# Truer durations in a build-time planner: layer norm, transposes, mixer output, normalisation products and TensorE's change of mode

## The chip, the core and the metric

The kernel runs on one core of one Trainium2 chip. The metric is the device time of one execution in microseconds. A timed comparison runs the two kernels in turn on the same chip.

## The reference, cut to what matters

Two layers, each an attention block followed by a token-mixing MLP, with S = 2048 tokens, D = 640 channels, 32 heads of 20 channels, F = 1536.

```python
x = x + A(layernorm(x), wqkv, wo)         # softmax(q k^T / sqrt(20)) v, then wo
x = x + B(layernorm(x), w1, b1, w2, b2)   # gelu over mixed tokens, residual
x = x + A(layernorm(x), wqkv, wo)         # the same weights again
x = x + B(layernorm(x), w1, b1, w2, b2)
```

## The kernel before

The instructions of each engine are not written down in an order. They are emitted by a greedy planner that runs while the program is built. It keeps a clock for each engine, gives every job a duration, and at each step emits the job that can start first on its engine. On the chip nothing of these clocks is left. What is left is the order in which each engine's instructions stand in the program, and the semaphores that they wait on.

```python
PE_MM = 216.0      # planned ns of one matmul of 512 columns
SW = 100.0         # planned ns for a change of TensorE's tiling mode
LAT_V = 120.0      # planned ns from VectorE's end to the reader
HAM_MIN = 10.0     # below this much recent matmul work, a hole gets a filler
...
def run_until(done):
    while not done():
        best = None
        for ch in (act_choose, dve_choose, pe_choose, pool_choose, sp_choose):
            c = ch()
            if c is not None and (best is None or c[0] < best[0]):
                best = c
        best[1](best[0])          # emits the instructions, advances that clock
```

The exponentials of the softmax are the largest work. They are cut in *units* of 128 keys x 512 queries x 4 heads, that is four *chunks* of 512 columns. ScalarE takes two or three chunks in one activation. The planner gives whole units to VectorE instead when it expects VectorE to finish them in time. VectorE then makes four *conversions* of scores and five *term passes*, whose results TensorE adds up.

```python
# ScalarE: n = 2 or 3 chunks
nc.scalar.activation(out=P[:, 0:n, :]..., in_=St[:, 0:n, :]..., func=ACT.Exp, scale=SCALE)
end = start + 67 + 426.7 * n
...
# VectorE: a conversion, and a term pass
nc.vector.tensor_scalar(out=c["jt"][:, j*512:(j+1)*512], in0=Dt[:], scalar1=..., scalar2=..., op0=ALU.mult, op1=ALU.add)
end = start + 600
...
nc.vector.tensor_scalar(out=tt_[:], in0=c["jt"][:], scalar1=0.5, scalar2=TERM_C[i], op0=ALU.mult, op1=ALU.add)
end = start + 605
...
# is one more unit worth giving to VectorE?
eta = (max(clk["DVE"], clk["PE"]) + (4 * 600.0 + NTERM * 610.0) * (d["open"] + 1) + len(t_jobs) * 610.0
       + sum(e[3] for e in jobs["DVE"]) + D_SLACK)
if eta <= act_end(si): ...
```

Where the planner sees a hole of over 250 ns on TensorE and little matmul work in the last 3.4 us, it emits a *filler*: a matmul with a zero weight, which adds nothing to an open accumulator. There are 362 fillers, 10 of them at the start.

TensorE works in three tiling modes: scores in four row groups, products with V and most others in four column groups, some at full size.

The softmax here doesn't subtract the row's maximum and nothing guards it: scores larger than these inputs give would overflow.

## Time and profile before

| | before |
|---|---|
| median of 4 runs | 1739.62 us (1738.45 to 1740.51) |
| span of the profiled execution | 1738.1 us |
| exponentials of layer 0, first start to last end | 782.3 us |
| change-over (mixer, next layer's start) | 50.2 us |
| exponentials of layer 1, first start to last end | 810.2 us |
| after the last exponential | 75.4 us |

From the profile's page: the span, the engines' busy time with its share of the span, and the chain of waits by engine.

```profile
span 1738.1 us, 50479 instructions
...
PE 1660.4 (96%) x21922; PEld 640.6 (37%) x21923; DVE 1463.7 (84%) x2613; ACT 1590.3 (91%) x1436; POOL 183.2 (11%) x297
...
PE 48%; ACT 21%; DVE 19%; issue 9%; DMA 2%; POOL 1%; DVEq 0%; POOLq 0%; SPq 0%; ACTq 0%
```

No engine stands out, so the averages must be split by stage. The next view is busy time in windows. The columns are: window and its width; busy us (and instructions) of PE, PEld, DVE, ACT, POOL; granted clock; DMA share; GB/s. The windows are layer 0's exponentials, the change-over, layer 1's first part (to the 37th accumulator transpose), layer 1's rest, and the tail.

```profile
20.00:802.30 782.30, 751.09 (x10025) 266.26 (x10018) 700.51 (x1227) 763.35 (x677) 84.07 (x117) 1.00 0.15 43
802.30:852.50 50.20, 47.07 (x475) 30.38 (x475) 28.08 (x66) 23.40 (x36) 6.70 (x20) 0.97 0.33 101
852.50:999.50 147.00, 142.16 (x2511) 69.53 (x2510) 73.67 (x146) 127.97 (x124) 12.05 (x27) 1.00 0.22 68
999.50:1662.70 663.20, 636.83 (x8317) 219.96 (x8314) 614.61 (x1064) 650.44 (x571) 68.63 (x96) 0.99 0.18 56
1662.70:1738.10 75.40, 69.04 (x517) 48.30 (x516) 33.35 (x70) 12.83 (x16) 3.66 (x12) 0.97 0.34 101
```

Read the width against ScalarE's busy time. Layer 0 leaves ScalarE idle for 782.30 - 763.35 = 18.95 us, layer 1's rest for 12.8 us. There ScalarE binds, and an idle microsecond of it is a microsecond of the kernel. In the change-over and layer 1's first part TensorE binds.

The durations that the change corrects stand in the groups by shape (mean ns of one after the comma):

```profile
L976 DVE STREAM_TRANSPOSE T_85<-pst 128x512 f32<-128x512 f32 x54 | 38.1, 705 | 2.6 <-PE pst L927 2.6
L1011 DVE STREAM_TRANSPOSE attnT<-T_86 128x256 f32<-128x256 f32 x62 | 26.6, 431 | 3.6 <-POOL T_86 L1001 3.5
L343 DVE BATCH_NORM_STATS2 bnst<-xs 128x6 f32<-128x320 f32 x40 | 19.1, 478 | 0.0
L1392 DVE SCALAR_TENSOR_TENSOR xs<-pst,b_t,xs 128x320 f32<-128x320 f32 x24 | 13.1, 550 | 34.0 <-PE pst L456 29.3 <-PE pst L453 3.3 <-DMA x2d<-xs 1.0
L530 DVE TENSOR_SCALAR attnT<-xs,mv,rt 128x640 bf16<-128x640 f32 x16 | 9.8, 612 | 7.9 <-POOL rt L356 7.8
L1001 POOL TENSOR_TENSOR T_86<-T_85,rden 128x512 bf16<-128x512 f32 x62 | 65.9, 1063 | 1132.7 <-DVE rden L988 1090.5 <-DVE attnT L1011 42.2
```

The cost of a change of mode shows in TensorE's timeline (start, duration of a run of matmuls, what ran):

```profile
1634.09 0.39 PE L700 MATMUL pst<-QT,KT 32*128 32x512 bf16 x2
1634.40 0.39 PE L927 MATMUL pst<-P,Vaug 128*32 128x512 bf16 x2
1634.41 0.39 PE L927 MATMUL pst<-JT,Vaug 128*32 128x512 bf16 x2
1634.63 0.85 PE L1065 MATMUL pst<-wo,attnT 128*32 128x320 bf16 x20
```

From the products at 1634.40 to the next group in the same mode is 0.23 us. From the scores at 1634.09 to the products, a change of mode, is 0.31 us. The difference is 0.08 us here. Over the whole trace, outside its half-clock stretches, the medians of the same two intervals are 225 and 321 ns, so a change of mode costs some 0.1 us.

### The profile page before, as it was taken

The page shows a single profiled execution, that of the slowest core. Times are in us where ns is not written, and L with a number is a line of the kernel's source. Part 1 is how long each engine was busy: PE and PEld are TensorE (multiplying, and loading weights), DVE is VectorE, ACT ScalarE, POOL GpSimd, SP SyncE. Part 2 cuts the span into 40 slices and gives each one's busy share as a digit, 9 for nine tenths or more (in the row PEclk, how much of TensorE's full clock was granted, in tenths as well). Part 3 has the DMA queues.
Part 4 walks back from the last instruction along what each step waited for, and adds up shares of the span by engine and source line. Part 5 has one row for each costly group of instructions (what it writes and reads, how often), then busy time and mean ns, then how long its engine had stood idle before and what let it go on. Part 6 is the DMA issues. An engine that isn't in the chain of part 4 may idle for free.

```text
span 1738.1 us, 50479 instructions
## 1 busy us (share of the span) xinstructions
PE 1660.4 (96%) x21922; PEld 640.6 (37%) x21923; DVE 1463.7 (84%) x2613; ACT 1590.3 (91%) x1436; POOL 183.2 (11%) x297
## 2 busy tenths in 40 slices
PE   8999999999999999998999999999999999999989
PEld 3433333323333333335545423332233333333356
DVE  6588999999988889997444699999999888889963
ACT  7899999999999999997598799999999999999950
POOL 3100002000300021001101000210002000300010
PEclk9999999999999999999999999999999999999999
DMA  3200001000121105610522000100002120266133
GB/s 118 29 2 2 2 13 36 1 1 2 52 70 56 38 32 178 191 47 28 162 84 68 15 2 2 39 24 2 2 19 69 56 64 24 78 192 198 63 99 96
DMA packets 103295, 98.06 MB, mean 56 GB/s; under 512 B 45600, under 2 KB 79520, under 8 KB 103072
## 3 DMA queue, kind: packets, MB, share of 16 engines
q1 hardware_dynamic: 99456, 94.82, 17.7%
q8 instruction: 171, 2.80, 0.7%
q0 software_dynamic: 3616, 0.01, 0.3%
q14 instruction: 52, 0.43, 0.1%
HBM read 63.35 MB, written 31.46 MB: 55 GB/s over the span
## 4 chain that ended last, share of the span: by engine, by line
PE 48%; ACT 21%; DVE 19%; issue 9%; DMA 2%; POOL 1%; DVEq 0%; POOLq 0%; SPq 0%; ACTq 0%
ACT P L887 21%; PE pst L700 14%; PE pst L927 13%; PE pst L456 12%; DVE JT L860 7%; DVE JT L840 6%; PE pst L453 5%; PE pst L1065 3%; DVE T_85 L976 1%; PE pst L1483 1%; DMA W<-in_B_w_dram 1%; DVE attnT L1011 1%; DVE QT L463 0%; DMA uacc_74<-W 0%; DVE xs L1094 0%
## 5 line engine op out<-in xcount | busy, mean ns | idle before, releaser
L887 ACT ACTIVATE P<-pst 128x1536 bf16<-128x1536 f32 (+1 forms) x1336 | 1523.5, 1294 | 31.4 <-PE pst L700 15.3
L860 DVE TENSOR_SCALAR JT<-JT 128x2048 uint16<-128x2048 uint16 x945 | 636.0, 706 | 3.9 <-PE pst L927 0.2
L700 PE MATMUL pst<-QT,KT 32*128 32x512 bf16 (+1 forms) x4224 | 589.8, 376 | 36.3 <-ACT P L887 26.5
L840 DVE TENSOR_SCALAR JT<-pst 128x512 uint16<-128x512 f32 x756 | 504.0, 678 | 81.1 <-PE pst L700 78.2
L927 PE MATMUL pst<-P,Vaug 128*32 128x512 bf16 (+1 forms) x3444 | 503.9, 380 | 3.7 <-ACT P L887 1.9
L927 PE MATMUL pst<-JT,Vaug 128*32 128x512 bf16 (+1 forms) x3900 | 464.0, 379 | 4.9 <-DVE JT L860 2.4
L700 PEld LDWEIGHTS <-KT 32*128 32x128 bf16 x4224 | 165.5, 91 | 504.5 <-issue 492.8
L927 PEld LDWEIGHTS <-Vaug 128*32 128x32 bf16 x7344 | 170.9, 94 | 307.1 <-issue 275.6
L1001 POOL TENSOR_TENSOR T_86<-T_85,rden 128x512 bf16<-128x512 f32 x64 | 67.7, 1057 | 1157.1 <-DVE rden L988 1114.9
L1065 PE MATMUL pst<-wo,attnT 128*32 128x320 bf16 x2048 | 108.1, 304 | 7.1 <-DVE attnT L1011 3.9
L1483 PE MATMUL pst<-ident,zw 128*32 128x512 bf16 (+1 forms) x352 | 113.5, 374 | 0.0
L456 PEld LDWEIGHTS <-W 128*32 128x32 bf16 x3384 | 91.0, 96 | 59.8 <-issue 27.7
L456 PE MATMUL pst<-hh,wq 128*32 128x512 bf16 x1232 | 102.2, 381 | 2.2 <-DVE JT L840 1.7
L456 PE MATMUL pst<-hh,wk 128*32 128x512 bf16 x1240 | 95.2, 381 | 1.3 <-DVE JT L840 0.6
L456 PE MATMUL pst<-x1last,W 128*32 128x320 bf16 x1536 | 81.5, 301 | 0.8 <-DVE JT L840 0.4
L1065 PEld LDWEIGHTS <-attnT 128*32 128x32 bf16 x2048 | 51.7, 96 | 49.1 <-issue 26.8
L456 PE MATMUL pst<-attnT,hh 128*32 128x320 bf16 x1196 | 61.4, 300 | 2.5 <-DVE JT L840 0.8
L456 PE MATMUL pst<-JT,W 128*32 128x320 bf16 x1080 | 51.8, 300 | 0.0
L456 PE MATMUL pst<-hh,W 128*32 128x320 bf16 x768 | 43.2, 304 | 5.1 <-DMA W<-in_B_w_dram 3.7
L463 DVE CAST KT<-pst 128x512 bf16<-128x512 f32 x51 | 34.7, 679 | 15.9 <-PE pst L456 14.6
L976 DVE STREAM_TRANSPOSE T_85<-pst 128x512 f32<-128x512 f32 (+1 forms) x58 | 39.9, 688 | 7.0 <-PE pst L927 7.0
L354 POOL TENSOR_SCALAR rt<-mv 128x1 f32<-128x1 f32 x64 | 13.0, 203 | 310.9 <-DVE mv L346 309.9
(92 smaller groups left out, 878.3 us busy)
## 6 DMA issues: line engine op xcount, KB each, us to landing
W<-in_B_w_dram SPq DMA_DIRECT2D x10, 768.0 KB
W<-in_B_w_dram SPq DMA_DIRECT2D x24, 256.0 KB
xs<-in_A_x_dram SPq DMA_DIRECT2D x32, 160.0 KB
x2d<-xs SPq DMA_DIRECT2D x16, 320.0 KB
xs<-x2d SPq DMA_DIRECT2D x16, 320.0 KB
x1d_69<-xs SPq DMA_DIRECT2D x12, 320.0 KB
uacca_72<-W SPq DMA_DIRECT2D x12, 320.0 KB
W<-uacca_72 SPq DMA_DIRECT2D x12, 320.0 KB
```

Source lines behind the costliest of these rows:

```text
L453: nc.tensor.matmul(out_, lhsT=lhsT, rhs=rhs, start=start, stop=stop)
L456: nc.tensor.matmul(out_[32 * c:32 * c + 32], lhsT=lhsT[:, 32 * c:32 * c + 32], rhs=rhs, start=start, stop=stop, tile_position=(0, 32 * c))
L463: nc.vector.tensor_copy(out=out_, in_=in_)
L700: pe(nc.tensor.matmul(dst, lhsT=k_, rhs=q_, start=True, stop=True, tile_position=(32 * j, 0)))
L840: nc.vector.tensor_scalar(out=c["jt"][:, j * 512:(j + 1) * 512], in0=Dt[:], scalar1=SCALE * LOG2E * 256.0, scalar2=127.0 * 256.0, op0=ALU. ...
L860: nc.vector.tensor_scalar(out=tt_[:], in0=c["jt"][:], scalar1=0.5, scalar2=TERM_C[i], op0=ALU.mult, op1=ALU.add)
L887: nc.scalar.activation(out=P[:, 0:n, :].rearrange("p a b -> p (a b)"), in_=St[:, 0:n, :].rearrange("p a b -> p (a b)"), func=ACT.Exp, scal ...
L927: pe(nc.tensor.matmul(dst, lhsT=Vaug[:, n:n + 32], rhs=ap, start=acc["cnt"][j] == 1 and not part, stop=last[j] and (half is None or part = ...
L976: nc.vector.transpose(out=T1[:], in_=src[:, 0:w])
L1001: eng.tensor_tensor(out=o_, in0=a_, in1=b_, op=ALU.mult)
L1065: nc.tensor.matmul(t[32 * c:32 * c + 32, 0:w], lhsT=q_, rhs=wo_pad[:, gg, c0:c1], start=(gi == 0), stop=(gi == len(gs) - 1), tile_position ...
L1483: pe(nc.tensor.matmul(dst[0:32, 0:128 * n], lhsT=zw[:, 0:32], rhs=ident[:].unsqueeze(1).to_broadcast([128, n, 128]), start=not inside, sto ...
```

## The change

The intent is a plan that is nearer to the chip, so that the emitted order fits better. No instruction's work changes. The diff, cut to its core:

```diff
-SW = 100.0
+SW = 105.0
...                                        # layer norm: statistics of a token tile
-            then(mv, start + 950 + LAT_V)
-        push("DVE", prio, ready, 950, f)
+            then(mv, start + 1030 + LAT_V)
+        push("DVE", prio, ready, 1030, f)
...                                        # layer norm: scaling (450 in both places before)
+                cost = 530 if L.x_in_dt == F32 else 400
...                                        # transpose of the accumulator
-                    acc["ready"] = start + 720 + LAT_V
+                    acc["ready"] = start + 740 + LAT_V
...                                        # normalisation product on GpSimd
-                        end_ = start + (600 if final else 1450)
+                        end_ = start + (600 if final else 1200)
...
-                        push("POOL", 0, start + 150 + LAT_V, 1300, f_mul, ok=lambda: len(rT2) > 0)
+                        push("POOL", 0, start + 170 + LAT_V, 1050, f_mul, ok=lambda: len(rT2) > 0)
...                                        # second transpose
-                        push("DVE", 3, end_, 340, f_tr2, ...)
+                        push("DVE", 3, end_, 360, f_tr2, ...)
...                                        # mixer output
-                    add_fill(mms, 136.0, evac, 450.0, pr=...)
+                    add_fill(mms, 136.0, evac, 470.0, pr=...)
```

## The prediction

> **What bounds the kernel now.** The page of the profile: span 1738.1 us, TensorE busy 96%, ScalarE 91%, VectorE 84%, GpSimd 11%, clock near full. The chain of waits: 48% TensorE, 21% ScalarE exponentials, 19% VectorE. By stage (busy time in windows, timeline of ScalarE):
> - attention of layer 0, 20 to 802 us: exponentials bind, 98 to 99% busy from 200 us on, about 19 us idle in all; TensorE is 96 to 98% busy, VectorE 86 to 99%.
> - mixer and the next layer's start, 802 to 852 us: TensorE binds (46 of 50 us).
> - layer 1's first 150 us: TensorE binds (95.5% at 900 to 1000 us; ScalarE idles 19 us there).
> - then exponentials again to 1663 us; last, 75 us of mixer tail, TensorE alone.
>
> **What the change does.** No arithmetic changes. A clock that exists only while the program is built orders instructions; it gets durations nearer to the trace's. By groups: statistics of a token tile 1.12 us end to end (0.95 becomes 1.03); scaling 0.61 us from float32, 0.44 from bf16 (0.45 becomes 0.53 or 0.40); normalisation product on GpSimd 1.06 us (1.30 becomes 1.05); transposes 0.705 and 0.43; mixer output 0.55 (0.45 becomes 0.47). Neighbours overlap, so intervals are about 0.08 us under these. Before a change of TensorE's mode a 0.22 us matmul slot lasts 0.32 in the timeline, so 105 ns is as right as 100. The Trainium skill, "TensorEngine Tiling (Array Packing)", Key Properties, says that a change of mode drains TensorE; the trace agrees (about 0.1 us).
>
> The corrections sum to little: 64 x 0.08 + 62 x 0.02 + 66 x 0.02 + 64 x 0.02 + 0.5 = about 9 us of planned VectorE time, 2750 x 0.005 = 14 us of planned TensorE time. Real durations do not move; only the order can pay.
>
> **What moves.** Comparing the two orders: ScalarE, GpSimd and SyncE keep 97 to 99% of theirs; VectorE keeps half in place and TensorE a third, by local swaps. In layer 1 one more unit of exponentials goes to VectorE (945 to 950 term passes, 756 to 760 conversions): ScalarE saves 4 x 0.43 = 1.7 us; VectorE gets 9 x 0.6 = 5.4 us, and has room. One term pass now stands just before the last accumulator transpose. TensorE loses 34 filler matmuls (362 to 328), 23 of them short ones of the last group: fewer planned holes. It makes 14 fewer mode changes, 1.4 us. At equal numbers of score chunks, its other work differs by a few us at most. No large shift to gain from.
>
> **On the critical path.** Layer 0: same split, -1 +-3 us. Transition: 0 +-2. Layer 1: -2 +-3 (the unit, the mode changes). Tail: 0, same order. Sum: about -3 us.
>
> **Predicted: 1736.5 us, range 1730 to 1743.** Faster by over 2%: 1%; within 2%: 98%; slower by over 2%: 1%.
>
> **What would show it.** Layer 0's last exponential (802.3 us) moves by under 4 us; 802 to 852 us by under 2; layer 1's exponentials (811 us, first to last) shorten by 1 to 5; the tail stays at 75 us. Mean durations of all groups stay. GpSimd's change shows nowhere.
>
> **What would make it wrong.** The order is greedy and sensitive: a late VectorE pass at a group's end can stall TensorE and ScalarE, several times, for 5 to 10 us. Real exponentials run 2.286 us a pair against 2.268 planned, uncorrected here, so the plan still drifts, which may hide any gain. The extra unit can come late and add 1 to 2 us.

## The result, and the profile after

| | before | after |
|---|---|---|
| median, first comparison | 1739.62 us (4 runs) | 1738.05 us (4 runs, 1736.88 to 1743.37) |
| ratio after to before | | 0.9997, 95% interval 0.9975 to 1.0019 |
| median, repeated in a later batch (experiment 1) | 1737.33 us (9 runs) | 1735.94 us (5 runs) |
| ratio | | 0.9996, 95% interval 0.9982 to 1.0009 |

A ratio is the mean time of one kernel's runs over that of the other's of the same rounds, so it is not quite the ratio of the medians. The change leaves the time as it was: both intervals hold 1.

The profiled execution after, from its page:

```profile
span 1735.1 us, 50465 instructions
...
PE 1647.8 (95%) x21920; PEld 645.9 (37%) x21921; DVE 1461.4 (84%) x2624; ACT 1584.5 (91%) x1433; POOL 180.2 (10%) x297
...
PE 43%; ACT 25%; DVE 20%; issue 11%; DMA 2%; POOL 1%; SPq 0%; ACTq 0%; POOLq 0%; DVEq 0%
```

The same five windows after:

```profile
20.50:806.90 786.40, 750.31 (x10026) 268.89 (x10019) 697.70 (x1227) 762.40 (x676) 81.11 (x117) 0.99 0.15 43
806.90:857.80 50.90, 47.02 (x475) 30.46 (x475) 28.13 (x67) 22.95 (x33) 7.32 (x20) 0.97 0.32 100
857.80:1003.60 145.80, 141.59 (x2505) 70.62 (x2504) 73.46 (x146) 126.69 (x123) 12.08 (x27) 1.00 0.22 69
1003.60:1659.00 655.40, 626.58 (x8311) 221.66 (x8312) 614.20 (x1071) 647.44 (x571) 65.43 (x92) 0.99 0.18 55
1659.00:1735.10 76.10, 67.98 (x527) 47.94 (x522) 34.01 (x73) 12.83 (x16) 5.99 (x16) 1.00 0.38 111
```

A net of nothing hides two movements of opposite sign. Layer 0 became 4.1 us longer: ScalarE's idle time there rose from 18.95 to 24.0 us. Layer 1 became 9.0 us shorter (147.0 + 663.2 before, 145.8 + 655.4 after). In its rest ScalarE idles 8.0 us instead of 12.8 and works 647.4 us instead of 650.4. The tail became 0.7 us longer, at a higher granted clock.

This is one trace of each kernel. They differ by 3.0 us, the timed medians only by 1.6 and 1.4 us. TensorE's clock differs too: the traces' clock records list stretches of 3.41 us at half clock (called *half-clock windows* below), and layer 0 has none of them before and three after. What they are worth is taken up in experiment 7 and after experiment 12.

Of the groups shown above, those of VectorE keep their means within 3 ns; the product on GpSimd went from 1063 to 1094 ns:

```profile
L977 DVE STREAM_TRANSPOSE T_85<-pst 128x512 f32<-128x512 f32 x54 | 38.3, 708 | 1.3 <-PE pst L928 1.2
L1012 DVE STREAM_TRANSPOSE attnT<-T_86 128x256 f32<-128x256 f32 x62 | 26.7, 434 | 5.4 <-POOL T_86 L1002 4.9
L530 DVE TENSOR_SCALAR attnT<-xs,mv,rt 128x640 bf16<-128x640 f32 x16 | 9.8, 612 | 8.3 <-POOL rt L356 7.9
L1002 POOL TENSOR_TENSOR T_86<-T_85,rden 128x512 bf16<-128x512 f32 x62 | 67.9, 1094 | 1123.8 <-DVE rden L989 1081.7 <-DVE attnT L1012 42.1
```

Not every group kept its mean: the scaling from bf16 went from 444 to 484 ns, the exponentials from 1505 to 1529 and from 1084 to 1106 ns. The interval between two exponentials that run back to back stayed at 1331 and 904 ns.

How the tail begins shows in the timelines of ScalarE and VectorE. A row merges neighbours, names the first one's shape, and its duration runs to the end of the last. Before:

```profile
1659.36 3.32 ACT L887 ACTIVATE P<-pst 128x1024 bf16<-128x1024 f32 x3
...
1660.76 0.21 DVE L346 BATCH_NORM_AGGREGATE mv<-bnst 128x2 f32<-128x12 f32 x1
1663.17 0.45 DVE L976 STREAM_TRANSPOSE T_85<-pst 128x256 f32<-128x256 f32 x1 [2.20 <-PE pst L927]
```

After:

```profile
1656.06 2.89 ACT L888 ACTIVATE P<-pst 128x1536 bf16<-128x1536 f32 x3
...
1659.37 0.64 DVE L861 TENSOR_SCALAR JT<-JT 128x2048 uint16<-128x2048 uint16 x1
1660.51 0.45 DVE L977 STREAM_TRANSPOSE T_85<-pst 128x256 f32<-128x256 f32 x1 [0.50 <-PE pst L928]
```

Before, the last exponential ends at 1662.68 and the last accumulator is transposed 0.49 us later; VectorE had been waiting. After, the last exponential ends at 1658.95, but a term pass of the extra unit on VectorE runs to 1660.01, TensorE must still use it, and the transpose starts 1.56 us after the exponential.

### The profile page after: what moved, and what is told of

It reads as the page before. It is cut to its first block, busy times and chain, and to the rows that moved or that the text cites. A ratio compares the mean times of both kernels' runs of the same rounds, so it can differ in the third digit from the quotient of the medians.

```text
span 1735.1 us, 50465 instructions
## 1 busy us (share of the span) xinstructions
PE 1647.8 (95%) x21920; PEld 645.9 (37%) x21921; DVE 1461.4 (84%) x2624; ACT 1584.5 (91%) x1433; POOL 180.2 (10%) x297
## 4 chain that ended last, share of the span: by engine, by line
PE 43%; ACT 25%; DVE 20%; issue 11%; DMA 2%; POOL 1%; SPq 0%; ACTq 0%; POOLq 0%; DVEq 0%
ACT P L888 24%; PE pst L701 12%; PE pst L928 11%; PE pst L456 11%; DVE JT L861 8%; DVE JT L841 7%; PE pst L453 5%; PE pst L1066 2%; DMA W<-in_B_w_dram 1%; DVE T_85 L977 1%; PE pst L1484 1%; DMA x2d<-xs 0%; PE pst L542 0%; DVE QT L463 0%; DVE attnT L1012 0%
## 5 line engine op out<-in xcount | busy, mean ns | idle before, releaser
L701 PE MATMUL pst<-QT,KT 32*128 32x512 bf16 (+1 forms) x4224 | 577.9, 377 | 48.9 <-ACT P L888 37.2
L841 DVE TENSOR_SCALAR JT<-pst 128x512 uint16<-128x512 f32 x760 | 509.5, 681 | 86.3 <-PE pst L701 83.4
L701 PEld LDWEIGHTS <-KT 32*128 32x128 bf16 x4224 | 173.0, 91 | 522.1 <-issue 509.8
L1002 POOL TENSOR_TENSOR T_86<-T_85,rden 128x512 bf16<-128x512 f32 x64 | 69.4, 1084 | 1146.4 <-DVE rden L989 1104.2
L1484 PE MATMUL pst<-ident,zw 128*32 128x512 bf16 (+1 forms) x318 | 106.9, 381 | 0.0
L456 PEld LDWEIGHTS <-wk 128*32 128x32 bf16 x1240 | 33.0, 95 | 33.7 <-issue 18.0
```

The costliest lines, as they stand in the source:

```text
L456: nc.tensor.matmul(out_[32 * c:32 * c + 32], lhsT=lhsT[:, 32 * c:32 * c + 32], rhs=rhs, start=start, stop=stop, tile_position=(0, 32 * c))
L701: pe(nc.tensor.matmul(dst, lhsT=k_, rhs=q_, start=True, stop=True, tile_position=(32 * j, 0)))
L841: nc.vector.tensor_scalar(out=c["jt"][:, j * 512:(j + 1) * 512], in0=Dt[:], scalar1=SCALE * LOG2E * 256.0, scalar2=127.0 * 256.0, op0=ALU. ...
L1002: eng.tensor_tensor(out=o_, in0=a_, in1=b_, op=ALU.mult)
L1484: pe(nc.tensor.matmul(dst[0:32, 0:128 * n], lhsT=zw[:, 0:32], rhs=ident[:].unsqueeze(1).to_broadcast([128, n, 128]), start=not inside, sto ...
```

## The experiments

Four theories were set against each other.

- *Accuracy*: a plan nearer to the truth runs faster. Then the parts of the change gain too, and wrong constants lose.
- *Units*: the time follows how many units VectorE takes off ScalarE, at 4 x 0.43 = 1.7 us each.
- *The draw*: any nudge of the planner gives another order. Its quality has no fixed relation to the truth of the constants, but it belongs to the order, so it repeats from run to run and from program to program.
- *The clock*: the new order has fewer fillers, and TensorE's granted clock falls to half more often.

The stage figures below are read from one trace for each program, as in the windows above; "layer 1" is from its first exponential's start to its last one's end. Experiments 1 to 4, 5 to 8 and 9 to 12 are three batches on three chips, each timed against before on its own chip; stage figures are compared across them.

### 1. after_again: the changed kernel once more

No edit.

> The changed kernel unchanged, for its scatter and a second trace. If the first trace's stages are a property of the order, the second trace shows layer 0's exponentials (first to last) 786 us plus or minus 2, layer 1's 801 plus or minus 2, and the fast runs average 0.15% below before (about 1737). If the scatter of the first four runs (1736.9 to 1743.4) is a property of the clock, the slower runs show the lower granted clock, and the two traces differ where half-clock spells fall.

Measured: ratio 0.9996 (0.9982 to 1.0009). Layer 0 784.3 us, layer 1 801.2 us. Its five runs are 1734.19 and 1734.23 (clock 0.992), 1735.94 and 1736.62 (0.992) and 1740.08 (0.988). The stages repeat: layer 0 is again longer than before's (by 2.0 us) and layer 1 shorter (by 9.0 us). How much of the loss in layer 0 is the clock's is taken up after experiment 12. The expected 0.15% is not shown; the interval allows it. The slowest run is the one of the lowest clock.

### 2 and 3. sw_alone and costs_alone: the change in two parts

```diff
 # sw_alone: before, and only
-SW = 100.0
+SW = 105.0
 # costs_alone: after, and only
-SW = 105.0
+SW = 100.0
```

> Only the change of mode at 105 ns. In the built program this gives two more units to VectorE than before (955 term passes). Theory of accuracy (a plan nearer the truth runs faster): between before and after, ratio 0.998 to 1.000. Theory of units (time follows ScalarE's chunks): layer sums of exponentials 2 x 1.7 us shorter, ratio 0.998. Theory of the draw (any nudge gives another order, good or bad by luck): anywhere in 0.996 to 1.004, no relation to the sum of the parts.

> All of the change but the mode cost (100 ns). 955 term passes as well. Accuracy: ratio 0.998 to 1.000, and together with sw_alone the two parts sum to the whole (0.9985 or so). Units: 0.998. Draw: 0.996 to 1.004, parts do not sum.

Measured: sw_alone 1.0012 (0.9994 to 1.0030), costs_alone 0.9994 (0.9979 to 1.0009). Both give VectorE two more units than before. For the theory of units both should have come to 0.998; sw_alone's interval excludes it. Layer 0 took 784.5 and 780.7 us, change-over and layer 1 together 858.1 and 854.5 us (before 860.4, after 852.1). The parts do sum to the whole within the scatter, so this pair doesn't speak for the draw. It doesn't separate accuracy from the draw either.

### 4. mirror: every constant as far off the other way

```diff
-SW = 100.0                                   +SW = 95.0
-  950 (statistics)                           +  870
-  450 / 450 (scaling, float32 / bf16)        +  370 / 500
-  720, 340 (transposes)                      +  700, 320
-  1300, end 1450 (product on GpSimd)         +  1550, end 1700
-  450 (mixer output)                         +  430
```

(The diff is abridged: each line stands for the places of the change's own diff.)

> Every constant of the change moved as far from before's value, the wrong way (statistics 870, product 1550, transposes 700 and 320, mixer output 430, mode 95 ns). The built program gives four more units to VectorE (965 term passes). Accuracy: slower than before, ratio 1.001 to 1.005. Units: four units less on ScalarE, up to 4 x 1.7 = 7 us, ratio 0.996. Draw: 0.996 to 1.004 without a sign.

Measured: 1.0015 (1.0001 to 1.0028). As a whole this is what accuracy expected, and far from the 0.996 of units. By stage it isn't so simple. Layer 0 took 778.6 us, the shortest of any order here. Change-over and layer 1 took 859.5 us, the tail 78.7 us, at a mean granted clock of 0.9905 over the four runs. The wrong constants made the better layer 0: two of the four units are taken off ScalarE there (1652 chunks instead of 1660 in the trace). Its activations, each at its back-to-back interval, sum to 738.1 us in layer 0 against before's 742.0, which is the whole of the 3.7 us. With the other two, change-over and layer 1 took 859.5 us against 860.4.

### 5. after_shadow: more fillers, nothing else moved

```diff
+        if o[0] > now + 250 and now > 2000 and a.want:       # a planned hole before the chosen job
+            return (o[0], lambda s_: (shadow(now, s_), o[3](s_)))
+    def shadow(now, s_):
+        ...                              # only into an open accumulator or a free bank
+        while t + 250 < s_ and sum(h[1] for h in hist) + len(sh) < 13.0:
+            pe(nc.tensor.matmul(dst[0:32, 0:128 * n], lhsT=zw[:, 0:32], ...))   # no planner clock is advanced
+            sh.append(t); t += 220
```

Apart from the fillers, all five engines' orders are identical to after's.

> The changed kernel with 173 more filler matmuls (328 to 501) in its planned holes of over 250 ns; every other instruction stands in the same order on every engine. Theory of the clock (the new order is worth about -2.5 us at equal clock, but its fewer fillers let the clock fall to half more often, and each spell of 3.4 us costs about 1 us): mean granted clock rises from 0.991 to at least 0.993, and the time falls by 1 to 3 us, ratio to before 0.997 to 0.9985. Rival, that fillers only cost TensorE its slots: clock as it was or higher, time longer by up to 173 x 0.22 = 38 us at worst, 2 to 5 us if most holes are real.

Measured: 0.9990 (0.9977 to 1.0003), granted clock 0.9940 on average of the five runs against 0.9912 in experiment 1. The clock rose as expected. The time (mean 1735.75 us against 1736.21) fell by less than the scatter, so the expected gain of 1 to 3 us is not shown.

### 6. before_shadow: the same for before

> The kernel before with 165 more fillers (362 to 527), same order otherwise. Clock theory: its clock is already 0.993, so it gains less than the changed kernel does, 0 to 2 us, ratio 0.999 to 1.000. If fillers only cost slots: slower, ratio above 1.001.

The edit is that of experiment 5, on the kernel before. Measured: 1.0031 (1.0018 to 1.0045), clock 0.9938, no higher than before's own 0.9936. With nothing to win on the clock, 165 fillers cost 1742.95 - 1737.20 = 5.75 us, or 35 ns each. The expectation of the theory of the clock missed the sign: it left out the fillers' price.

### 7. after_nofill: no fillers

```diff
 def do_warm(start):
     ...
-    pe(nc.tensor.matmul(dst[0:32, 0:128 * n], lhsT=zw[:, 0:32], ...))
     if not inside: ...                     # the planner's clock goes on as before
```

> The changed kernel without any of its 318 fillers after the start, same order otherwise. Clock theory: the granted clock falls, to 0.985 or lower, and the time rises by about 1.06 us for each 0.001 of the clock, so by 6 us or more. If fillers only cost slots: the clock may fall, but the time does not rise, or falls.

Measured: 1.0024 (1.0006 to 1.0042), mean clock 0.9837. Against experiment 1 the clock fell by 0.0075 and the time rose by 1741.71 - 1736.21 = 5.5 us. So low clock does cost time, and the fillers earn more than their slots. The rise is a little under the expected 6 us, as it would be if the freed slots gave some back.

The scatter says the same. Over the 87 runs here that list a clock, with a level of its own for each kernel in each batch, a least-squares line gives about 0.96 us for each 0.001 of mean clock. The trace's clock records show TensorE at half clock for single windows of 3.41 us, or two to three in a row. One window is 0.5 x 3.41 / 1735 = 0.001 of the mean clock, so by this line it costs about 1 us. The stages agree: after_nofill has after's order, and its layer 0 took 791.2 us with eight half-clock windows, after_again's 784.3 us with one, that is 6.9 us for seven windows.

### 8. exp_true: the largest duration made true as well

In the traces ScalarE's exponentials start every 1331 ns (three chunks) and 904 ns (two chunks) where they run back to back, by the median. The plan has 1347 and 920.

```diff
-EXP_CH = 453.0                              +EXP_CH = 447.0
-    end = start + 67 + 426.7 * n            +    end = start + 51 + 426.7 * n
```

> The change, and the exponentials' planned time set to the interval that the traces show (904 and 1331 ns instead of 920 and 1347). The plan is nearer the truth in its largest term, and gives ScalarE two units more than after (940 term passes). Accuracy: faster than after, ratio to before 0.995 to 0.998. Units: four chunks more a unit, two units, +3.5 us on after, ratio 1.001 to 1.002. Draw: 0.996 to 1.004.

Measured: 1.0099 (1.0082 to 1.0116), 17 us slower than before. This is the strongest blow to accuracy: the most important constant, made true, gave the slowest kernel of all. Two units fewer on VectorE explain at most 3.5 us. The trace shows layer 0 at 790.8 us, change-over and layer 1 at 860.6 us and the tail at 81.4 us. About 4 us of the loss are the clock's by the line of experiment 7 (mean clock 0.9895 against before's 0.9936 in the batch). In the tail the last accumulator's transpose starts 6.16 us after the last exponential, in before's 0.48 us after it. The rest stays open.

### 9. exp_slack: the largest duration further off

```diff
-EXP_CH = 453.0                              +EXP_CH = 459.0
-    end = start + 67 + 426.7 * n            +    end = start + 83 + 426.7 * n
```

> The change, with exponentials planned 16 ns longer than in it, so 32 ns longer than they are. VectorE gets five more units (975 term passes). The run with the true interval was 17 us slower than before. If slack in the plan is what pays: ratio 0.994 to 0.999. If it is VectorE's share: 5 units x 1.7 us, ratio 0.995, with ScalarE's sum of back-to-back intervals 9 us shorter but its losses as in after. If the draw: 0.997 to 1.010.

Measured: 1.0054 (1.0036 to 1.0071). Slack doesn't pay, and the theory of units is refuted as a rule for the whole time. VectorE took five more units, and ScalarE's back-to-back intervals (each activation at its median) sum to 736.6 + 745.6 us against 742.0 + 749.2 after. But what the layers took beyond that sum rose from 44.4 + 51.9 to 52.7 + 70.4 us. That is not the clock's doing: the trace has no half-clock window in layer 0 and one in layer 1, where after's has three and two. The tuned value of the constant, which is not the true one, beats both neighbours.

### 10, 11 and 12. hyb_ba, hyb_ab and hyb_ma: one set of constants for each layer

The planner's constants are switched when it turns to layer 1:

```diff
+KS = (layer_0_constants, layer_1_constants)
+PH = [0]
+def kc(n):
+    return KS[PH[0]][n]
...
-            then(mv, start + 1030 + LAT_V)
+            then(mv, start + kc("st") + LAT_V)
...                                                     # likewise for the others
+        PH[0] = 1
         state.att = L1
```

hyb_ba has before's constants for layer 0 and the change's for layer 1. hyb_ab has them the other way round. hyb_ma has mirror's for layer 0 and the change's for layer 1. Comparing the built programs shows that VectorE's order in a layer follows that layer's constants: the same as that of before, after or mirror in layer 0, and 99.4 to 100% of that of before or after in layer 1. So orders can be put together like parts.

> Before's constants while layer 0 is planned, the change's while layer 1 is. In the built program VectorE's order in layer 0 is exactly before's, in layer 1 the changed kernel's (99.9%). If a stage's time belongs to its order: layer 0's exponentials 782 us (first to last), layer 1's 801, and the whole about 3 us below the changed kernel and 5 to 8 below before, ratio 0.9955 to 0.998. If the gain of layer 1 in the changed kernel is only layer 0's loss given back (a shift of the clock's spells or of DMA landings): layer 1 805 us or more, ratio 0.999 to 1.001.

> The other way round: the change's constants for layer 0, before's for layer 1; VectorE's order is exactly after's in layer 0 and before's in layer 1. If a stage's time belongs to its order: layer 0 785 us, layer 1 810, whole 2 to 4 us above before, ratio 1.001 to 1.0025. Otherwise within 0.1% of before.

> The wrong-way constants (mirror) for layer 0, the change's for layer 1: orders exactly mirror's and 99.4% after's; 960 term passes. If a stage's time belongs to its order and not to how true its constants are: layer 0 779 us, layer 1 801, whole 8 to 11 us below before, ratio 0.9935 to 0.996, faster than the change in both layers though half its constants are the more wrong. If truth of constants pays: slower than hyb_ba.

Measured: hyb_ba 0.9966 (0.9949 to 0.9984), hyb_ab 1.0028 (1.0009 to 1.0047), hyb_ma 0.9953 (0.9936 to 0.9971). The windows of hyb_ba:

```profile
19.50:801.30 781.80, 751.04 (x10025) 266.48 (x10018) 701.17 (x1228) 763.26 (x677) 84.44 (x118) 1.00 0.15 43
801.30:852.20 50.90, 47.08 (x476) 30.38 (x475) 28.32 (x67) 22.95 (x33) 6.61 (x19) 0.97 0.32 100
852.20:997.50 145.30, 141.85 (x2504) 70.52 (x2504) 72.93 (x145) 127.28 (x124) 12.03 (x27) 1.00 0.22 69
997.50:1652.20 654.70, 627.29 (x8307) 221.30 (x8311) 613.19 (x1070) 647.48 (x571) 64.99 (x91) 0.99 0.18 55
1652.20:1730.10 77.90, 69.64 (x531) 48.76 (x527) 34.70 (x74) 13.11 (x17) 6.31 (x17) 0.97 0.37 109
```

Of hyb_ab, the two long windows:

```profile
19.80:806.30 786.50, 750.09 (x10026) 269.54 (x10023) 698.11 (x1229) 762.23 (x676) 81.50 (x118) 0.99 0.15 43
...
1003.60:1663.90 660.30, 634.37 (x8313) 219.50 (x8314) 614.41 (x1063) 650.23 (x571) 68.64 (x96) 1.00 0.18 56
```

Of hyb_ma, the windows without the tail:

```profile
20.00:800.00 780.00, 746.15 (x10047) 264.84 (x10040) 706.41 (x1239) 762.06 (x677) 81.61 (x113) 1.00 0.15 43
800.00:846.60 46.60, 42.30 (x362) 27.54 (x357) 30.09 (x70) 19.56 (x28) 9.38 (x23) 0.93 0.36 109
846.60:999.00 152.40, 149.03 (x2658) 74.71 (x2659) 73.89 (x146) 130.82 (x130) 12.07 (x27) 1.00 0.21 66
999.00:1655.30 656.30, 628.86 (x8314) 221.92 (x8312) 613.66 (x1071) 647.45 (x571) 65.26 (x91) 0.99 0.18 55
```

Sorted by order instead of by kernel:

| order | layer 0, us | order | rest of layer 1, us |
|---|---|---|---|
| before's | 782.3, hyb_ba 781.8 | before's | 663.2, hyb_ab 660.3 |
| after's | 786.4, 784.3, hyb_ab 786.5 | after's | 655.4, 655.5, hyb_ba 654.7, hyb_ma 656.3 |
| mirror's | 778.6, hyb_ma 780.0 | mirror's | 656.3 |

The stages travel with their orders. But these lengths hold half-clock windows, and stages are compared fairly only when these are counted. The table takes 1 us off for each, an estimate from experiment 7. Layer 1 is here the whole of it; hyb_ma's, which began earlier, is left out.

| order | layer 0, us | windows | less 1 us each | layer 1, us | windows | less 1 us each |
|---|---|---|---|---|---|---|
| before's (layer 0: before, hyb_ba; layer 1: before, hyb_ab) | 782.3, 781.8 | 0, 0 | 782.3, 781.8 | 810.2, 807.4 | 2, 0 | 808.2, 807.4 |
| after's (after, after_again; then hyb_ab or hyb_ba) | 786.4, 784.3, 786.5 | 3, 1, 3 | 783.4, 783.3, 783.5 | 801.1, 801.2, 800.0 | 2, 3, 2 | 799.1, 798.2, 798.0 |
| mirror's (mirror, hyb_ma) | 778.6, 780.0 | 1, 2 | 777.6, 778.0 | | | |

So by this estimate the order explains little over 1 us of the 4.1 us that layer 0 lost in the profiled pair, and three windows the rest. Mirror's advantage is its two units. The gain in layer 1, some 9 us, is not the clock's. Places of windows recur (near 738 us in after, after_again and after_shadow) but not in every trace, so it isn't shown how far the windows belong to the order.

The whole times followed: hyb_ba and hyb_ma fell in the expected ranges, and hyb_ab came out a little slower than its range (1.001 to 1.0025). The rival, that layer 1's gain is only layer 0's loss given back, expected hyb_ba at 0.999 to 1.001 and is refuted. hyb_ma also shows a miss in what was expected: its layer 1 was to take 801 us and took 152.4 + 656.3 = 808.7 us. Its exponentials began earlier (change-over 46.6 us instead of the 50.9 of hyb_ba), and the part in which TensorE binds then took 152.4 us instead of 145.3. Change-over and first part together are 199.0 us against hyb_ba's 196.2.

Two kernels beat before: hyb_ba by 0.3% and hyb_ma by 0.5%. The changed kernel did not run in their batch; hyb_ma's interval lies below that of experiment 1 (0.9982 to 1.0009), hyb_ba's just touches it. Half of hyb_ma's constants are the wrong-way ones. Between the two the intervals overlap, so it isn't shown which is the better.

## Why the prediction was right, and where it was not

The median of the predicted comparison was 1738.05 us, inside the range of 1730 to 1743 us, and "within 2%" was right. The main reasons hold. The instructions' work did not change; the corrections sum to little; only the order could pay; and no stage moved by more than some 9 us. But the sum was right partly by luck, because two of its terms missed in opposite directions. ("Mean durations of all groups stay" is not quite so either, as the groups after show.)

- *"Layer 0: same split, -1 +-3 us."* Wrong in sign as measured. After's order took 784.3 to 786.5 us in three traces, before's 781.8 and 782.3. ScalarE's idle time in it was 18.5 and 19.0 us in before's order and 22.2 to 24.3 us in after's. The split was the same, as predicted. What the prediction left out is the clock: at equal half-clock windows the order costs little over 1 us by the estimate above, inside the stated range, and the rest of the loss in the profiled pair is three windows.
- *"Transition: 0 +-2."* Right: 50.2 against 50.9 us.
- *"Layer 1: -2 +-3 (the unit, the mode changes)."* Right in sign, too small: 801.1, 801.2 and 800.0 us in the traces of after's order, 810.2 and 807.4 in those of before's. The unit was sized well: ScalarE's busy time in the rest fell by 3.0 us, where four chunks account for 1.7. What was missing is 4.8 us less idle time of ScalarE, which no count of units or mode changes shows. The share of the 14 saved mode changes (1.4 us as predicted) was not measured apart.
- *"Tail: 0, same order."* The prediction also named the risk that the extra unit comes late and adds 1 to 2 us. That happened: from the last exponential to the last transpose is 0.5 us in three traces of before's layer-1 order (before, before_shadow, hyb_ab) and 1.6 to 1.9 us in four of after's (after, after_again, after_shadow, hyb_ba). This term should have stood in the sum and not among the risks.
- *"Fewer planned holes"* was the prediction's reading of the 34 missing fillers. It was read as a gain only. The other side is the clock: 0.9931 for before and 0.9912 for after in the same batch. At 0.96 us for each 0.001 this is an estimate of 1.8 us lost. Putting fillers back raised the clock but did not measurably shorten the time (experiment 5), so that estimate is consistent with the runs and not shown by them.
- *"Real exponentials run 2.286 us a pair against 2.268 planned."* Wrong. It looks like a merged row of the timeline divided by its pairs (8 activations in 9.14 us give 2.285); such a row's duration includes the last activation's overlap. Start to start a pair takes 1.331 + 0.904 = 2.235 us, so the plan is too slow and not too fast. The step "uncorrected here, so the plan still drifts, which may hide any gain" fails as well: correcting it made the kernel 1% slower.

What a lost microsecond looks like can be followed in one place. The Trainium skill, "Perfetto Trace Analysis", Optimization Strategy, says to look for the gaps on the engine that binds within its regime and ask what blocks there. In before, ScalarE's timeline near the end of layer 1 has this gap:

```profile
1591.90 2.61 ACT L887 ACTIVATE P<-pst 128x1536 bf16<-128x1536 f32 x2
1597.20 2.37 ACT L887 ACTIVATE P<-pst 128x1536 bf16<-128x1536 f32 x2 [2.69 <-PE pst L927]
```

and hyb_ab, whose layer 1 has the same order, has it at the same exponential:

```profile
1592.36 4.84 ACT L895 ACTIVATE P<-pst 128x1536 bf16<-128x1536 f32 x4
1598.43 2.37 ACT L895 ACTIVATE P<-pst 128x1536 bf16<-128x1536 f32 x2 [1.24 <-PE pst L935]
```

ScalarE waits for TensorE's products with V (the named line). At this point in before VectorE is handing over a finished group's accumulator (transpose at 1592.46 us), and TensorE works off its backlog before ScalarE gets a buffer back. Counted as the delay of this exponential beyond its back-to-back interval, it is 3.07 us in before, 2.66 us in before_shadow and 1.61 us in hyb_ab. Their layer-1 order is the same but for before_shadow's fillers; what differs is the clock. The windows of the delay in before and in hyb_ab (the granted clock is the third number from the end):

```profile
1594.13:1597.20 3.07, 3.07 (x29) 0.84 (x30) 3.07 (x5) 0.38 (x2) 0.52 (x1) 0.51 1.13 303
1596.82:1598.43 1.61, 1.61 (x30) 0.57 (x23) 1.61 (x3) 0.37 (x1) 0.52 (x1) 1.00 1.13 288
```

before_shadow is at half clock there too. In after's order the exponential of the same rank is late by 0.98 us in after, again with a half-clock window over it, and by 0.15 us at most in after_again, after_shadow and hyb_ba, at full clock. So at full clock the order is worth some 1.5 us at this place, and a half-clock window that falls on it adds 1.1 to 1.5 us. Why the truer constants removed this wait was not traced step by step and stays open; so does the rest of exp_true's 17 us.

Which theory stands? Units fails as a rule (experiments 2 and 9), though two units' saving does show in mirror's layer 0. Accuracy fails as a rule: experiment 8 made the largest constant true and lost 1%, and hyb_ma, with wrong-way constants in layer 0, is faster than the change (in another batch). The clock explains much of the scatter and, by the estimate above, most of layer 0's loss, but not layer 1's gain. For layer 1 the draw stands: the order's quality belongs to the order and repeats, but could not be read from the truth of the constants.

## What to carry to other kernels

When a plan is built from modelled durations, a truer duration is a new order and not a gain; judge it by the stages of its trace as well as by the whole time, because gains and losses of several microseconds cancel. Count each stage's half-clock windows before a difference is put down to the order; here they made most of one. If the stages are planned apart, take the better order for each: here two unchanged sets of constants, switched between layers, gave 0.3 to 0.5% where the change as a whole gave nothing. Take an interval from start to start before you feed it to a model, and try the true figure before trusting it: here the tuned one beat it by 1%.

## What the Trainium skill lacked or had wrong

- "TensorE: Matmul & The Clock Gate", Part 1: The HAM clock gate, describes a free-running window of 3413 ns and two clock rates, full and half. The traces agree: every half-clock spell inside the kernel is one to a few windows of 3.41 us, on one fixed grid in each trace. The page's table gives an idle window as the reason for the lower rate; further on the page also blames short idle times between groups of matmuls, without a figure. Here the window before a spell was not idle: in four traces (before, after, hyb_ba, hyb_ab) TensorE's matmuls filled 32 to 70% of it, and some windows of 52 to 70% had no spell after them. So no single share of filling separates the two, and the page gives none.
- The same page has no price for fillers. Here 165 of them, where the clock had nothing to win, cost 35 ns each (experiment 6), and leaving out all 318 cost 5.5 us (experiment 7).
- "TensorEngine Tiling (Array Packing)", Key Properties, says that a change of tiling mode drains TensorE and gives no duration. The timeline shows about 0.1 us (0.31 against 0.23 us from one group's start to the next; medians of the trace 321 against 225 ns).
- No page says how far a modelled schedule should follow measured durations; here the true interval of the exponentials, 16 ns below the tuned one, cost 1.0%.
